# The float64 weights' conversion in an attention, experts and gated layer kernel: other steps, other buffers, other engines for its low part

## The chip, the cores and the metric

One NeuronCore of a Trainium2 chip runs the whole program. The metric is the device time of one execution in microseconds (us); the median of several is compared. The engines are PE (TensorE, matmuls; PEld is its weight load), DVE (VectorE), ACT (ScalarE), POOL (GpSimd) and SP (SyncE, which here only issues transfers). Each works through its own queue in order.

## What is computed

Three layers follow each other: attention with a window of 32 (in half of the heads with a stride of 4), a mixture of eight experts of which each of the 2304 tokens uses two, and a gated layer.

```python
def reference(**kwargs):
    ...
    attn_out = _attn_ref(**attn_kwargs)
    B, H, S, D = attn_out.shape
    x = np.ascontiguousarray(attn_out.transpose(0, 2, 1, 3)).reshape(B * S, H * D)
    x = _moe_ref(x=x, **moe_kwargs)
    return _moe2_ref(x=x, **moe2_kwargs)

def _moe2_ref(x, w_gate, w_val, w_out):
    g = x @ w_gate
    silu = g * (1.0 / (1.0 + np.exp(-g)))
    val = x @ w_val
    return (silu * val @ w_out).astype(np.float32)
```

The gated layer's three weights (512 x 1536 twice and 1536 x 512) arrive as float64. Every fp32 product is made of float32r parts: a high and a low one of each operand, and three matmuls.

## The kernel before

The order of the work is written by hand: each engine's queue holds its instructions in the order in which the program issues them. Attention comes first (36 units), then the expert layer, then the gated layer.

**The expert layer's steps.** `segs` cuts the experts' slots into 11 segments of 256, 256, 384, 384, five times 640, 384 and 256 slots; each has 8 steps, one for each 128 of the hidden columns, so there are 88 steps, and `moe_step(i)` issues one. Steps 16 to 31 are the segments of 384 slots, steps 32 to 71 the five of 640, steps 72 to 79 the next of 384. In a step

- SP loads the raw weights for step i+5 (line 156). There are three raw buffers, so this load waits until `wlo` of step i+2 is made.
- PE makes the first product (line 636) into bank A (steps of 640 slots have this one bank; those of 384 use A and B in turn), and then the second product of step i-1 (line 675).
- ACT makes hhi, the high part of the first product (line 648), then DVE makes hlo (line 649). The next step's first product needs the bank that both read.
- ACT makes whi (line 162) and DVE wlo (line 164), the weights' parts for step i+2.
- In the first steps of a segment POOL gathers rows of x for the next one (line 579, four gathers a step), and from its third step on, one block in each, DVE turns a block (line 585, "the transpose"), ACT makes xth (line 599) and DVE xtl (line 601). A segment of 640 slots has five such steps.

**The conversion.** The float64 weights are turned into float32r parts beside the expert layer, in 36 blocks of 128 x 512. From step 32 (`CV0`) on each step runs one `cv_tick(t)`, which does six stages for six blocks: load r (SP, line 739); clear what is below the least normal number (ACT three times, lines 753 to 756, and a POOL product, line 757, which gives cvw); one tick later cv_parts, four bit operations on DVE, which cut the 32-bit words into h, the high part, and c, the next bits (lines 763 to 766); then cv_hi: two more DVE operations (u, the power of two of h, line 772, and c with that exponent, line 773), ACT's copy hr of h (line 774) and SP's store of hr (line 778); then cv_sub: POOL makes c - u (line 794); then cv_lo: ACT's copy lr, scaled (line 784), and SP's store (line 788). The ticks run in steps 32 to 74. The conversion's pool lies on the right side of SBUF, where the routing's pool was until step 31. The stored parts are loaded again for the gated layer from step 80 on (`load_w2`, line 725).

Of the kernel before, what the change touches and what calls it, by code (L numbers as in the profile page):

```python
# [20 lines left out]
N, DM, E, FF, F2 = 2304, 512, 8, 1024, 1536  # L21
NT = N // 128          # token tiles
NB = S // 64           # query blocks of one sequence
SEG = S // 4           # positions of one residue class
NA = N // 128          # most slot blocks of one expert
CAP = 640              # slots of one expert on the straight path
EARLY = 256            # first slots of experts 0 and 1, filled by batches 0 and 1 only
LOW = 384              # tokens of one block of the last layer
ID0 = 1024
# [11 lines left out]
def attn_moe_glu_kernel(ctx, tc, qT, kT, vB, cst, wgn, noise, wm, wz, out):  # L41
# [16 lines left out]

    # rows of x by token, then rows of y by slot (block, expert, row); a token with a slot past the
    # straight path finds its combined row in the place of its x  # L60
    zd = dr.tile([N + NA * E * 128, DM], F32, name="zd")
# [21 lines left out]

    # ------------------------------------------------------------ loads
    qt, kt, vt = {}, {}, {}
# [12 lines left out]

    # dense work for the array while the first loads are on their way
    fill = gp.tile([128, 512], BF16, tag="g_ob", bufs=1, name="fill")  # L100
# [43 lines left out]

    # ------------------------------------------------------------ expert weights
    segs = [(0, 0, EARLY), (1, 0, EARLY), (0, EARLY, CAP), (1, EARLY, CAP)] \
# [18 lines left out]

    # ------------------------------------------------------------ attention
    units = []
# [63 lines left out]
    def pieces(subs):  # L231
        """(partition, type, first token, step, count) of the rows of a unit"""
        res = []
        for sub, (t, j) in enumerate(subs):
            p = j * 64
            while p < j * 64 + 64:
                if t == 0:
                    n = j * 64 + 64 - p
                    tok, st = p, 1
                else:  # L240
                    n = min(j * 64 + 64, (p // SEG + 1) * SEG) - p
                    tok, st = 4 * (p % SEG) + p // SEG, 4
                q0 = sub * 64 + p - j * 64
                if res and res[-1][1] == t and res[-1][2] + res[-1][4] * st == tok:
                    res[-1][4] += n
                else:
                    res.append([q0, t, tok, st, n])
                p += n
        return res
# [32 lines left out]

    # ------------------------------------------------------------ gating and routing
    groups = [(0, 4), (4, 9), (9, 13), (13, 18)]
# [7 lines left out]
    def regroup(o, src):  # L292
        """row 32 t + c of src to the rows 32 g + c of o's part t, for all g"""
        for t in range(4):
            T.matmul(o[:, t, :], lhsT=sel[:, t, :], rhs=src,
                     start=True, stop=True, skip_group_check=True)
# [244 lines left out]

    # the routing's small instructions, a few at a time between other work
    NEXT = "next"
# [22 lines left out]

    # ------------------------------------------------------------ expert layers
    xgt, xth, xtl, hps, hh_, hl_, yps = {}, {}, {}, {}, {}, {}, {}

    # column 4 p + k of a row belongs on partition p of chunk k: either PE turns a block of rows, or the  # L570
    # rows come in quarters, quarter g of the tokens 32 t + c on partition 32 g + c, and DVE turns 32 x 32
    def quarters(z):
# [8 lines left out]
    def turned(g, quarter, o=None):  # L581
        """a block of rows with its columns on partitions, [partition, chunk, row]"""
        if quarter:
# [10 lines left out]
    def parts(src, hi, lo, quarter, eng=V):  # L594
        """its two parts, on ACT and then on another engine"""
        how = "p k (t q) -> p k t q" if quarter else "p (k t) q -> p k t q"
# [92 lines left out]

    # ------------------------------------------------------------ emission: attention  # L690
    def att_step(i, turn):
# [3 lines left out]
        if i in FIRST_X:  # L695
            # the score bank has room for it
            tx = trans_x(0, FIRST_X.index(i), sT[i + 1][:, :, 192:448].rearrange("p a (c q) -> p a c q", c=2))
            next(tx)
# [32 lines left out]

    # the gated layer's weights, split once into two float32r parts
    cs = [{} for _ in range(3 * NK)]
# [14 lines left out]
    def cv_zero(n):  # L748
        if wide:
# [3 lines left out]
            A.activation(f, w1.bitcast(F32), AF.Abs)  # L753
            # 1 from the least normal number on, else 0
            A.activation(f, f, AF.Relu, scale=-2.0 ** 40, bias=least[0])
# [3 lines left out]
    def cv_parts(n):  # L759
        if wide:  # L760
            w0, w1 = cs[n]["r"][:, 0:1024:2], cs[n]["w"]
            h, c = cv_tile(n, "h", 2), cv_tile(n, "c", 3)
            V.tensor_scalar(h, w1, 3, 0x3FFFF000, op0=OP.logical_shift_left, op1=OP.bitwise_and)
            V.tensor_scalar(c, w1, 14, 0x7FC000, op0=OP.logical_shift_left, op1=OP.bitwise_and)
            V.scalar_tensor_tensor(h, w1, -0x40000000, h, op0=OP.bitwise_and, op1=OP.bitwise_or)
            V.scalar_tensor_tensor(c, w0, 18, c, op0=OP.logical_shift_right, op1=OP.bitwise_or)

    def cv_hi(n):
        hr = cv_tile(n, "hr", 2 if wide else 3, F32R)
        if wide:  # L770
            u, c, h = cv_tile(n, "u", 3), cs[n]["c"], cs[n]["h"]
            V.tensor_scalar(u, h, -0x800000, None, op0=OP.bitwise_and)
            V.scalar_tensor_tensor(c, h, -0x800000, c, op0=OP.bitwise_and, op1=OP.bitwise_or)
            A.activation(hr, h.bitcast(F32), AF.Copy)
        else:
            A.activation(hr, cs[n]["r"], AF.Copy)
        f, q = divmod(n, 3)
        SP.dma_start(whd[f, :, q * 512:q * 512 + 512], hr.bitcast(F32))

    def cv_lo(n):  # L780
        lr = cv_tile(n, "lr", 2, F32R)
        if wide:
            u = cs[n]["u"].bitcast(F32)
            A.activation(lr, u, AF.Copy, scale=2.0 ** -11)
        else:
            V.tensor_tensor(lr, cs[n]["r"], cs[n]["hr"].bitcast(F32), op=OP.subtract)
        f, q = divmod(n, 3)
        SP.dma_start(wld[f, :, q * 512:q * 512 + 512], lr.bitcast(F32))
        cs[n] = None

    def cv_sub(n):
        if wide:
            u, c = cs[n]["u"].bitcast(F32), cs[n]["c"].bitcast(F32)
            G.tensor_tensor(u, c, u, op=OP.subtract)

    def cv_tick(t):
        for d, fn in ((6, cv_lo), (5, cv_sub), (4, cv_hi), (3, cv_parts), (2, cv_zero), (0, cv_load)):
            if 0 <= t - d < 3 * NK:
# [34 lines left out]
    DVE_SEGS = (3, 11)  # L833
    CV0 = 32
    least = []
    pools = {}

    def moe_step(i):
        s, f = steps[i]
        last = s == len(segs) - 1  # L840
        load_raw(i + 5)
        if i == CV0:
            cv = pools["cv"] = st_cv.enter_context(tc.tile_pool(name="cv", bufs=1, side="right", reuse_waits="tile"))
            least.append(cv.tile([128, 1], F32, name="least"))
# [41 lines left out]
        go(5)  # L886
        if i == CV0 - 1:
            assert not route
            st_gate.close()
        if CV0 <= i:  # L890
            if i <= CV0 + 3 * NK + 6:
                cv_tick(i - CV0)
                if i == CV0 + 3 * NK + 6:
                    st_cv.close()
        list(tx)
# [37 lines left out]

    # ------------------------------------------------------------ emission: experts
    route.append([routing(3), True])
# [7 lines left out]

    # ------------------------------------------------------------ slots past the straight path
    rv = nc.values_load(most[0:1, 0:1], min_val=0, max_val=NA)
    with tc.If(rv > CAP // 128):  # L946
        with tc.tile_pool(name="ov", bufs=1) as ov:
            # rows that no expert computes
            none = ov.tile([128, E, DM], F32, name="none")
# [48 lines left out]

    # ------------------------------------------------------------ gated layer
    wp = ctx.enter_context(tc.tile_pool(name="wp", bufs=1))  # L1000
# [4 lines left out]
    def glu_gv(i):  # L1005
        b, f = st2[i]
        xh, xl = x2t[b]
        p = gvp[i] = bank2("AB"[i % 2])
        # what comes last from DVE or DRAM is used last
        parts = [(wh2[f], xh), (wh2[f], xl), (wl2[f], xh)] if i else [(wh2[f], xh), (wl2[f], xh), (wh2[f], xl)]  # L1010
# [19 lines left out]
    def glu_out(i):  # L1030
# [10 lines left out]
        if f == NK - 1:  # L1041
            for j in range(3):
                # the very last rows leave in two halves
                cut = (0, 256, 512) if b == NBLK - 1 and j == 2 else (0, 512)
# [111 lines left out]
```

## Time and profile before

| | |
|---|---|
| runs | 1083.07, 1078.17, 1081.59 us; median 1081.59 |
| the profiled execution | its span is 1085.7 us, 17127 instructions; no other time is given for it |
| PE busy | 1030.4 us (95%) |
| DVE busy | 667.9 us (62%) |
| ACT busy | 486.7 us (45%) |
| POOL busy | 441.3 us (41%) |
| chain that ended last | PE 42%, with all others under half a per cent |

The shares are means over the three layers, which have different limits, so the expert layer has to be read by itself: by windows of time, by the waits in it, and by the starts of an instruction that comes once in each step. Times in the trace are counted from the span's start. A row of the timeline gives start, duration, engine, line and operation, and in brackets the idle time of the engine before it and what ended it. A line of the page that sums instructions gives their count, the total and the mean in ns. An operation that stands behind a lock counts as busy.

### The profile page before, as it was taken

The numbers are of one execution on the slowest core, as the hardware profiler recorded it, in microseconds if no ns is written. First come the engines' busy times: TensorE is split into PE (matmuls) and PEld (weight loads), VectorE is DVE, ScalarE is ACT, GpSimd is POOL, SyncE is SP. The second block draws the span as 40 slices with busy tenths as digits, with TensorE's granted clock in tenths as the row PEclk, the third lists the DMA queues.
The fourth block names the chain that finished last, engine by engine and source line by source line (L and its number), as shares of the span: only waits on it lengthen the run. The fifth ranks groups of instructions, "written<-read, shape, count | busy, mean of one in ns | idle before, by whom it ended". The sixth has DMA issues, their size and how long they took to land. (4 is left out here: it accounts for less than half of the span.)

```text
span 1085.7 us, 17127 instructions
## 1 busy us (share of the span) xinstructions
PE 1030.4 (95%) x6561; PEld 923.5 (85%) x6562; DVE 667.9 (62%) x1223; ACT 486.7 (45%) x909; POOL 441.3 (41%) x389
## 2 busy tenths in 40 slices
PE   7888989999998888988999999999999999999998
PEld 5676779999987877877789899999999999999997
DVE  3468777674999999998995634434335344244222
ACT  4666644454767766676664422223223222122111
POOL 0014156741688576785761247724315116000000
PEclk9888999999999998998999999999999999999999
DMA  7777346654577676775769668511101101100000
GB/s 234 222 225 231 109 141 217 190 180 157 186 237 240 201 263 190 248 250 185 247 202 327 185 221 293 193 49 27 54 11 37 42 10 43 36 1 1 30 1 29
DMA packets 59526, 161.34 MB, mean 149 GB/s; under 512 B 10032, under 2 KB 16560, under 8 KB 58672
## 3 DMA queue, kind: packets, MB, share of 16 engines
q1 hardware_dynamic: 46736, 121.27, 35.0%
q0 software_dynamic: 12560, 38.82, 11.0%
q8 instruction: 52, 0.85, 0.3%
q14 instruction: 34, 0.28, 0.1%
q10 hardware_dynamic: 144, 0.13, 0.0%
HBM read 121.37 MB, written 38.80 MB: 148 GB/s over the span
## 5 line engine op out<-in xcount | busy, mean ns | idle before, releaser
L579 POOL DMA_INDIRECT yg<-zd,row x126 | 124.6, 989 | 200.8 <-DVE yg L820 117.4
L579 POOL DMA_INDIRECT xg<-zd,idx x139 | 163.9, 1179 | 58.5 <-issue 32.5
L636 PE MATMUL bA<-xth,whi 128*128 128x320 f32 (+2 forms) x452 | 119.2, 322 | 32.6 <-DVE hlo L649 32.4
L164 DVE TENSOR_TENSOR wlo<-raw,whi 128x1024 fp32r<-128x1024 f32 x80 | 112.7, 1408 | 12.9 <-ACT whi L162 12.8
L636 PEld LDWEIGHTS bA<-xth,whi 128*128 128x128 f32 x452 | 80.9, 194 | 46.0 <-DVE hlo L649 43.0
L636 PE MATMUL bA<-xtl,whi 128*128 128x320 f32 (+2 forms) x452 | 115.9, 315 | 0.0
L636 PE MATMUL bA<-xth,wlo 128*128 128x320 f32 (+2 forms) x452 | 115.7, 314 | 0.0
L1023 DVE TENSOR_TENSOR t<-bB,ex 128x384 f32<-128x384 f32 x36 | 20.1, 557 | 134.4 <-ACT ex L1021 134.4
L162 ACT ACTIVATE whi<-raw 128x1024 fp32r<-128x1024 f32 x88 | 92.7, 1053 | 3.4 <-DMA raw<-in_wm 3.4
L757 POOL TENSOR_TENSOR cvw<-r,cvw 128x512 f32<-128x512 f32 x36 | 58.5, 1625 | 84.8 <-issue 46.9
L648 ACT ACTIVATE hhi<-bA 128x640 fp32r<-128x640 f32 (+2 forms) x73 | 42.2, 578 | 98.4 <-PE bA L636 98.1
L636 PEld LDWEIGHTS bA<-xtl,whi 128*128 128x128 f32 x452 | 81.0, 194 | 1.2 <-DVE xtl L601 0.2
L636 PEld LDWEIGHTS bA<-xth,wlo 128*128 128x128 f32 x452 | 80.5, 193 | 0.0
L649 DVE SCALAR_TENSOR_TENSOR hlo<-bA,hhi 128x640 fp32r<-128x640 f32 (+2 forms) x73 | 48.6, 666 | 51.9 <-ACT hhi L648 51.9
L1027 ACT ACTIVATE th<-t 128x384 fp32r<-128x384 f32 x72 | 37.8, 524 | 90.3 <-DVE t L1024 90.3
L1021 ACT ACTIVATE ex<-bB 128x384 f32<-128x384 f32 x36 | 17.7, 492 | 135.0 <-PE bB L1015 135.0
L1023 DVE TENSOR_TENSOR t<-bA,ex 128x384 f32<-128x384 f32 x36 | 19.9, 554 | 83.5 <-ACT ex L1021 83.5
L1028 DVE TENSOR_TENSOR tl<-t,th 128x384 fp32r<-128x384 f32 x72 | 40.3, 559 | 42.6 <-ACT th L1027 42.6
L599 ACT ACTIVATE xth<-xg 128x512 fp32r<-128x512 f32 x33 | 38.0, 1152 | 63.4 <-DVE xg L585 63.4
L1015 PE MATMUL bA<-x2h,wh 128*128 128x384 f32 x288 | 56.6, 338 | 0.5 <-PEq L946 0.3
L1021 ACT ACTIVATE ex<-bA 128x384 f32<-128x384 f32 x36 | 17.7, 492 | 87.6 <-PE bA L1015 86.5
L1015 PE MATMUL bB<-x2h,wh 128*128 128x384 f32 x288 | 56.4, 337 | 0.0
(232 smaller groups left out, 2639.2 us busy)
## 6 DMA issues: line engine op xcount, KB each, us to landing
raw<-in_wm SPq DMA_DIRECT2D x88, 512.0 KB, 4.2
r<-in_wz SPq DMA_DIRECT2D x36, 512.0 KB, 5.9
zd<-y SPq DMA_DIRECT2D x40, 256.0 KB, 5.4
whd<-cvhr SPq DMA_DIRECT2D x36, 256.0 KB, 4.7
wld<-cvlr SPq DMA_DIRECT2D x36, 256.0 KB, 4.7
wh<-whd POOLq DMA_DIRECT2D x12, 768.0 KB, 8.6
wl<-wld POOLq DMA_DIRECT2D x12, 768.0 KB, 8.8
v<-in_vB SPq DMA_DIRECT2D x8, 877.5 KB, 8.7
```

The source lines that it names most:

```text
L162: A.activation(whi[i], raw[i], AF.Copy)
L164: eng.tensor_tensor(wlo[i], raw[i], whi[i].bitcast(F32), op=OP.subtract)
L579: G.indirect_dma_start(out=g, out_offset=None, in_=src, in_offset=bass.IndirectOffsetOnAxis(ap=ix, axis=0))
L599: A.activation(hi, src, AF.Copy)
L636: T.matmul(hp[:, q, 0:cw], lhsT=wt[:, ws], rhs=xt[:, c, q * cw:q * cw + cw], start=c == 0 and j == 0, stop=c == 3 and j == 2)
L648: A.activation(a3, hp, AF.Relu)
L649: V.scalar_tensor_tensor(l3, hp, 0.0, a3.bitcast(F32), op0=OP.max, op1=OP.subtract)
L757: G.tensor_tensor(f, w1.bitcast(F32), f, op=OP.mult)
L1015: T.matmul(p[:, q, 0:LOW], lhsT=w[:, ws], rhs=x[:, c, :], start=c == 0 and j == 0, stop=c == 3 and j == 2, skip_group_check=True)
L1023: V.tensor_tensor(t, p[:, 0, 0:LOW], ex, op=OP.mult)
L1027: A.activation(a, t, AF.Copy)
L1028: V.tensor_tensor(l, t, a.bitcast(F32), op=OP.subtract)
```

## The change

The conversion does the same for each block with other instructions. Five bit operations on DVE, all in cv_parts: u is made there, and c keeps its bits as an integer. cv_hi no longer copies h: h itself is stored, and ACT turns c into a float, scaled (cf). cv_lo multiplies cf by u on POOL and writes lr; its store moves to a stage of its own, one tick later, cv_end. h has three buffers in place of two, c two in place of three. The ticks are spread: the first five lie in steps 17, 20, 23, 26 and 29, the other 38 in steps 32 to 76, five in each six steps (there is none in 35, 41, 47, 53, 59, 65 and 71). The pool moves to the left side of SBUF, where the attention's was.

```diff
     def cv_parts(n):
         if wide:
             w0, w1 = cs[n]["r"][:, 0:1024:2], cs[n]["w"]
-            h, c = cv_tile(n, "h", 2), cv_tile(n, "c", 3)
+            h, c, u = cv_tile(n, "h", 3), cv_tile(n, "c", 2), cv_tile(n, "u", 3)
...
+            V.tensor_scalar(u, h, -0x800000, None, op0=OP.bitwise_and)
     def cv_hi(n):
-        hr = cv_tile(n, "hr", 2 if wide else 3, F32R)
         if wide:
-            u, c, h = cv_tile(n, "u", 3), cs[n]["c"], cs[n]["h"]
-            V.tensor_scalar(u, h, -0x800000, None, op0=OP.bitwise_and)
-            V.scalar_tensor_tensor(c, h, -0x800000, c, op0=OP.bitwise_and, op1=OP.bitwise_or)
-            A.activation(hr, h.bitcast(F32), AF.Copy)
+            hr = cs[n]["h"].bitcast(F32)
+            cf = cv_tile(n, "f", 2, F32)
+            A.activation(cf, cs[n]["c"], AF.Copy, scale=2.0 ** -34)
...
-        SP.dma_start(whd[f, :, q * 512:q * 512 + 512], hr.bitcast(F32))
+        SP.dma_start(whd[f, :, q * 512:q * 512 + 512], hr)
     def cv_lo(n):
         lr = cv_tile(n, "lr", 2, F32R)
         if wide:
-            u = cs[n]["u"].bitcast(F32)
-            A.activation(lr, u, AF.Copy, scale=2.0 ** -11)
+            G.tensor_tensor(lr, cs[n]["f"], cs[n]["u"].bitcast(F32), op=OP.mult)
...
+    def cv_end(n):
         f, q = divmod(n, 3)
-        SP.dma_start(wld[f, :, q * 512:q * 512 + 512], lr.bitcast(F32))
+        SP.dma_start(wld[f, :, q * 512:q * 512 + 512], cs[n]["lr"].bitcast(F32))
         cs[n] = None
-    def cv_sub(n):
-        if wide:
-            u, c = cs[n]["u"].bitcast(F32), cs[n]["c"].bitcast(F32)
-            G.tensor_tensor(u, c, u, op=OP.subtract)
+    CV_LAST = 6
     def cv_tick(t):
-        for d, fn in ((6, cv_lo), (5, cv_sub), (4, cv_hi), (3, cv_parts), (2, cv_zero), (0, cv_load)):
+        for d, fn in ((CV_LAST, cv_end), (5, cv_lo), (4, cv_hi), (3, cv_parts), (2, cv_zero), (0, cv_load)):
...
-    CV0 = 32
+    CVS = [17, 20, 23, 26, 29] + [32 + round(1.2 * j) for j in range(3 * NK + CV_LAST - 4)]
...
-        if i == CV0:
-            cv = pools["cv"] = st_cv.enter_context(tc.tile_pool(name="cv", bufs=1, side="right", reuse_waits="tile"))
+        if i == CVS[0]:
+            cv = pools["cv"] = st_cv.enter_context(tc.tile_pool(name="cv", bufs=1, reuse_waits="tile"))
...
-        if CV0 <= i:
-            if i <= CV0 + 3 * NK + 6:
-                cv_tick(i - CV0)
-                if i == CV0 + 3 * NK + 6:
-                    st_cv.close()
+        if i in CVS:
+            cv_tick(CVS.index(i))
+            if i == CVS[-1]:
+                st_cv.close()
```

First place: DVE's queue in a step of 640 slots that has a transpose and a block. Before:

```order
L649 SCALAR_TENSOR_TENSOR hlo<-bA,hhi 128x640
L585 STREAM_TRANSPOSE xg<-xg 128x4x4x32
L772 TENSOR_SCALAR cvu<-cvh 128x512
L773 SCALAR_TENSOR_TENSOR cvc<-cvh,cvc 128x512
L763 TENSOR_SCALAR cvh<-cvw 128x512
L764 TENSOR_SCALAR cvc<-cvw 128x512
L765 SCALAR_TENSOR_TENSOR cvh<-cvw,cvh 128x512
L766 SCALAR_TENSOR_TENSOR cvc<-r,cvc 128x512
L601 TENSOR_TENSOR xtl<-xg,xth 128x4x128
L164 TENSOR_TENSOR wlo<-raw,whi 128x1024
L649 SCALAR_TENSOR_TENSOR hlo<-bA,hhi 128x640
```

The same place with the change, with step 35 ahead of it, which has no tick:

```order
L649 SCALAR_TENSOR_TENSOR hlo<-bA,hhi 128x640
L585 STREAM_TRANSPOSE xg<-xg 128x4x4x32
L601 TENSOR_TENSOR xtl<-xg,xth 128x4x128
L164 TENSOR_TENSOR wlo<-raw,whi 128x1024
L649 SCALAR_TENSOR_TENSOR hlo<-bA,hhi 128x640
L585 STREAM_TRANSPOSE xg<-xg 128x4x4x32
L764 TENSOR_SCALAR cvh<-cvw 128x512
L765 TENSOR_SCALAR cvc<-cvw 128x512
L766 SCALAR_TENSOR_TENSOR cvh<-cvw,cvh 128x512
L767 SCALAR_TENSOR_TENSOR cvc<-r,cvc 128x512
L768 TENSOR_SCALAR cvu<-cvh 128x512
L601 TENSOR_TENSOR xtl<-xg,xth 128x4x128
```

A block has one DVE instruction less, and all five belong to the same block; step 35 has none.

Second place: DVE's queue at step 26, of 384 slots, with the change (before, xtl is followed by hlo at once):

```order
L649 SCALAR_TENSOR_TENSOR hlo<-bA,hhi 128x384
L585 STREAM_TRANSPOSE xg<-xg 128x4x4x32
L164 TENSOR_TENSOR wlo<-raw,whi 128x1024
L601 TENSOR_TENSOR xtl<-xg,xth 128x4x128
L764 TENSOR_SCALAR cvh<-cvw 128x512
L765 TENSOR_SCALAR cvc<-cvw 128x512
L766 SCALAR_TENSOR_TENSOR cvh<-cvw,cvh 128x512
L767 SCALAR_TENSOR_TENSOR cvc<-r,cvc 128x512
L768 TENSOR_SCALAR cvu<-cvh 128x512
L649 SCALAR_TENSOR_TENSOR hlo<-bB,hhi 128x384
```

The first block's five instructions stand ahead of step 27's hlo; the second block's stand likewise at step 29.

Third place: POOL's queue in two steps with gathers, before:

```order
L794 TENSOR_TENSOR cvu<-cvc,cvu 128x512
L757 TENSOR_TENSOR cvw<-r,cvw 128x512
L579 DMA xg<-zd,idx_86 128x128 x4
L794 TENSOR_TENSOR cvu<-cvc,cvu 128x512
L757 TENSOR_TENSOR cvw<-r,cvw 128x512
```

and with the change:

```order
L785 TENSOR_TENSOR cvlr<-cvf,cvu 128x512
L757 TENSOR_TENSOR cvw<-r,cvw 128x512
L579 DMA xg<-zd,idx_86 128x128 x4
L785 TENSOR_TENSOR cvlr<-cvf,cvu 128x512
L757 TENSOR_TENSOR cvw<-r,cvw 128x512
```

The product for lr stands where the subtraction stood, ahead of the one that gives cvw.

## Rows read from the trace of the kernel before

**Rows 1.** Windows: us, busy of PE, PEld, DVE, ACT, POOL, clock, DMA, GB/s

```profile
400.00:500.00 100.00, 86.35 (x450) 77.25 (x451) 96.38 (x116) 65.36 (x95) 69.21 (x53) 0.93 0.68 220
420.00:440.00 20.00, 15.56 (x74) 14.18 (x73) 17.23 (x23) 10.57 (x16) 8.91 (x6) 0.83 0.54 165
```

**Rows 2.** Waits from 280 to 565 us: total, times, longest

```profile
PEld bA L636 <- DVE hlo L649: 38.0, 22, 4.9
```

**Rows 3.** DVE line 649 (hlo): its forms, then starts in the timeline

```profile
L649 DVE SCALAR_TENSOR_TENSOR hlo<-bA,hhi x73: 409/809/826, 123.8 to 620.0; 128x640 fp32r<-128x640 f32 x40, 128x256 fp32r<-128x256 f32 x18, 128x384 fp32r<-128x384 f32 x15
...
264.16 0.82 DVE L649 SCALAR_TENSOR_TENSOR hlo<-bA,hhi 128x640 fp32r<-128x640 f32 x1 [4.77 <-ACT hhi L648]
...
284.98 0.82 DVE L649 SCALAR_TENSOR_TENSOR hlo<-bA,hhi 128x640 fp32r<-128x640 f32 x1 [0.21 <-ACT hhi L648]
...
374.15 0.81 DVE L649 SCALAR_TENSOR_TENSOR hlo<-bA,hhi 128x640 fp32r<-128x640 f32 x1
...
440.24 0.82 DVE L649 SCALAR_TENSOR_TENSOR hlo<-bA,hhi 128x640 fp32r<-128x640 f32 x1 [1.81 <-ACT hhi L648]
...
562.58 0.81 DVE L649 SCALAR_TENSOR_TENSOR hlo<-bA,hhi 128x640 fp32r<-128x640 f32 x1
```

**Rows 4.** Groups by line on DVE, 200 to 285 us, mostly without conversion

```profile
L164 DVE TENSOR_TENSOR wlo<-raw,whi 128x1024 fp32r<-128x1024 f32 x17 | 20.6, 1213 | 2.5 <-ACT whi L162 2.3
L585 DVE STREAM_TRANSPOSE xg<-xg 128x512 f32<-128x512 f32 x9 | 10.0, 1116 | 0.0
L601 DVE TENSOR_TENSOR xtl<-xg,xth 128x512 fp32r<-128x512 f32 x9 | 9.7, 1072 | 2.1 <-ACT xth L599 1.5
...
L765 DVE SCALAR_TENSOR_TENSOR cvh<-cvw,cvh 128x512 int32<-128x512 int32 x2 | 1.4, 683 | 0.0
...
L764 DVE TENSOR_SCALAR cvc<-cvw 128x512 int32<-128x512 int32 x2 | 0.8, 418 | 0.0
```

**Rows 5.** Groups by line on DVE, 280 to 560 us, beside the conversion

```profile
L164 DVE TENSOR_TENSOR wlo<-raw,whi 128x1024 fp32r<-128x1024 f32 x34 | 56.7, 1666 | 0.0
L601 DVE TENSOR_TENSOR xtl<-xg,xth 128x512 fp32r<-128x512 f32 x21 | 32.7, 1558 | 0.0
L766 DVE SCALAR_TENSOR_TENSOR cvc<-r,cvc 128x512 int32<-128x512 int32 x34 | 30.9, 910 | 0.0
L772 DVE TENSOR_SCALAR cvu<-cvh 128x512 int32<-128x512 int32 x35 | 29.2, 834 | 0.0
...
L773 DVE SCALAR_TENSOR_TENSOR cvc<-cvh,cvc 128x512 int32<-128x512 int32 x35 | 27.0, 773 | 0.0
L765 DVE SCALAR_TENSOR_TENSOR cvh<-cvw,cvh 128x512 int32<-128x512 int32 x34 | 25.3, 745 | 0.0
L764 DVE TENSOR_SCALAR cvc<-cvw 128x512 int32<-128x512 int32 x35 | 25.0, 715 | 0.0
...
L763 DVE TENSOR_SCALAR cvh<-cvw 128x512 int32<-128x512 int32 x35 | 14.8, 423 | 0.0
```

**Rows 6.** Timeline, DVE's wlo and POOL's two products in the same 4 us

```profile
386.80 3.98 DVE L164 TENSOR_TENSOR wlo<-raw,whi 128x1024 fp32r<-128x1024 f32 x1
...
387.11 1.31 POOL L794 TENSOR_TENSOR cvu<-cvc,cvu 128x512 f32<-128x512 f32 x1
...
388.36 1.32 POOL L757 TENSOR_TENSOR cvw<-r,cvw 128x512 f32<-128x512 f32 x1
```

**Rows 7.** Timeline of the same step: ACT's hhi, PE's last matmul of the second product

```profile
387.94 0.70 ACT L648 ACTIVATE hhi<-bA 128x640 fp32r<-128x640 f32 x1 [3.70 <-PE bA L636]
...
390.94 0.39 PE L675 MATMUL bf<-whi,hlo 128*128 128x512 f32 x1
```

**Rows 8.** Timeline, hlo of steps 27 and 28 (384 slots)

```profile
229.14 0.56 DVE L649 SCALAR_TENSOR_TENSOR hlo<-bB,hhi 128x384 fp32r<-128x384 f32 x1 [0.35 <-ACT hhi L648]
...
233.33 0.56 DVE L649 SCALAR_TENSOR_TENSOR hlo<-bA,hhi 128x384 fp32r<-128x384 f32 x1 [0.30 <-ACT hhi L648]
```

**Rows 9.** Tile of lr: its 36 stores' time from issue to landing

```profile
DMA to landing us min/median/max: 4.1/4.7/13.8
```

More of the change, by code (lines that the diff above doesn't have):

```diff
@@ L766, in cv_parts @@
             V.scalar_tensor_tensor(c, w0, 18, c, op0=OP.logical_shift_right, op1=OP.bitwise_or)
+            V.tensor_scalar(u, h, -0x800000, None, op0=OP.bitwise_and)
     def cv_hi(n):
-        hr = cv_tile(n, "hr", 2 if wide else 3, F32R)
+        f, q = divmod(n, 3)
         if wide:
-            u, c, h = cv_tile(n, "u", 3), cs[n]["c"], cs[n]["h"]
-            V.tensor_scalar(u, h, -0x800000, None, op0=OP.bitwise_and)
-            V.scalar_tensor_tensor(c, h, -0x800000, c, op0=OP.bitwise_and, op1=OP.bitwise_or)
-            A.activation(hr, h.bitcast(F32), AF.Copy)
+            hr = cs[n]["h"].bitcast(F32)
+            cf = cv_tile(n, "f", 2, F32)
+            A.activation(cf, cs[n]["c"], AF.Copy, scale=2.0 ** -34)
         else:
+            hr = cv_tile(n, "hr", 3, F32R)
             A.activation(hr, cs[n]["r"], AF.Copy)
-        f, q = divmod(n, 3)
-        SP.dma_start(whd[f, :, q * 512:q * 512 + 512], hr.bitcast(F32))
+            hr = hr.bitcast(F32)
+        SP.dma_start(whd[f, :, q * 512:q * 512 + 512], hr)
     def cv_lo(n):
@@ L886, in moe_step @@
         go(5)
-        if i == CV0 - 1:
+        if i == 31:
             assert not route
             st_gate.close()
-        if CV0 <= i:
-            if i <= CV0 + 3 * NK + 6:
-                cv_tick(i - CV0)
-                if i == CV0 + 3 * NK + 6:
-                    st_cv.close()
+        if i in CVS:
+            cv_tick(CVS.index(i))
+            if i == CVS[-1]:
+                st_cv.close()
         list(tx)
```

## Prediction

> **What bounds the kernel now.** I read four views in this order. First the windows: between 400 and 500 us DVE is busy for 96.38 of 100 us and PE for 86.35, and in the 20 us from 420 the granted TensorE clock has a mean of 0.83 [rows 1]. So in this stage the array is not the limit; its clock even falls to 1.2 GHz for a part of it, after PE has been waiting. Second the waits: what PE's weight loads wait for there is hlo, the last DVE instruction before the next step's matmuls, 38.0 us in 22 waits [rows 2]. Third, the starts of hlo on DVE, one per step [rows 3]. The row of forms says that there are 40 steps of 640 slots (steps 32 to 71); the last starts at 562.58, and the row at 284.98 is the sixth, step 37. From 264.16 to 284.98 three steps take 20.82 us, 6.94 each: that is PE's own pace. From step 37 to step 71 there are 34 steps in 277.6 us, where 34 x 6.94 is 236.0. **The excess is 41.6 us**, and it is all that a relief of DVE can give back here. The lower clock is a part of it. Behind this stage the chain of waits is PE alone, so time saved here reaches the end.
>
> Fourth, the price of DVE's instructions, without and with the conversion. Alone (200 to 285 us) wlo takes 1213 ns, the transpose 1116, xtl 1072, a one-tensor bit operation 418 and a two-tensor one 683 [rows 4]. Beside the conversion the means are 1666 for wlo, 1558 for xtl, and up to 910 for the bit operations [rows 5]. One row shows why: a wlo of 3.98 us has two GpSimd TENSOR_TENSORs of 1.31 and 1.32 us inside it [rows 6], and 1.21 + 2.63 is 3.84. Summed over rows 5 (mean less the time alone, times count) DVE loses 64 us in 34 blocks, each with two such GpSimd operations: 0.94 us for each. I call this the lock.
>
> The Trainium skill (SBUF — State Buffer, "SBUF: two separate sides") says that DVE and GpSimd share one pair of ports as an exclusive lock, held for a whole instruction, while the other fully blocks. Rows 6 agree with it.
>
> **The change, part by part.** *DVE.* A block had six bit operations and has five: line 773 leaves, 35 times 773 ns, 27.0 us [rows 5]. Of 36 blocks, six no longer lie in steps 35 to 71, but in 26, 29, 32, 33, 34 and 72. The other five groups of rows 5 sum to 125.2 us for 35 blocks, 3.58 each: 21.5 us more leaves the slow stage. Together that is 48.5, more than 41.6, so on the average DVE stops being the limit. If a step were an average, all 41.6 us would go.
>
> It isn't. hlo of a step can't start before PE has made that step's first product, so an idle DVE can't work ahead; it can only be late, by some 1.9 us, before PE stands: ACT's hhi ends at 388.64, hlo would be done 0.82 later, and PE has work until 391.33 [rows 7]. So I count steps with a transpose and a block: 0.82 + 1.12 + 1.07 + 1.21 + 3 x 0.42 + 2 x 0.68 = 6.84 us, and two locks. With the old block this rule gives 6.84 + 0.68 + 1.88 = 9.40, 2.46 over 6.94; five in a row less the 1.9 are 10.4 us per expert. Measured from 374.15 to 440.24, eight steps, is 66.1 less 55.5: 10.6 [rows 3]. The rule holds.
>
> Now for the new order. The pause of one step in six falls on 35, 41, 47, 53, 59, 65 and 71; steps three to seven of an expert have the transpose (three steps for the last of the five). So experts 4, 6 and 7 each have a run of three such steps (36 to 38, 50 to 52, 60 to 62) and single ones that the 1.9 us hides; the one at steps 64 to 71 has a run of three; the one at 40 to 47 has its pauses outside and five in a row. For the lock I take 0.8: a little under 0.94, because DVE now stands idle in the pauses and in the steps without a transpose, where an operation on GpSimd costs nothing. Each such step is then 6.84 + 1.6 - 6.94 = 1.5 over. Three in a row leave 4.5 - 1.9 = 2.6, five leave 5.6: 4 x 2.6 + 5.6 = **16 us stay**. With 0.94 it is 20.8, with 0.6 it is 9.2.
>
> *Two early blocks* at steps 26 and 29, in the 384-slot steps with a transpose. DVE has only 0.35 us of idle time in such a step of 4.19 us [rows 8]. A block and a lock put it 2.62 + 0.8 - 0.35 = 3.07 behind. With two banks in turn hlo is wanted later, by the end of the next first product: 4.19 less hhi (0.70 in its 640 form, rows 7, so no more) less 0.56 is 2.9 us of room. The first block loses 0.2; three steps win back 1.05, and the second block brings 3.07 again: 2.0. **2.2 us lost**, between 1.8 and 3.2 by locks of 0.6 and 1.31. The blocks at 32 to 34 cost nothing: at step 34 DVE stands idle for 4.77 us [rows 3].
>
> *ACT* makes one conversion (cf) in place of two copies (hr, lr): less by one copy a block, off the path, zero. That an int32 input costs the same I bound by zero and by one copy more, which would be the work of before. *GpSimd* keeps two TENSOR_TENSORs a block; the new one multiplies where the old one subtracted, and the two kinds in rows 6 take 1.31 and 1.32, so its own cost is unchanged. *SP* issues the same transfers; whd waits for a DVE instruction of the step before instead of ACT's copy, and the five early loads are passed by raw loads with room to spare. *Other buffers*: the conversion's space is that of the attention, long finished at step 17; zero.
>
> **Sum:** 41.6 - 16 - 2.2 = 23.4 us less. The profiled span is 1085.7, 4.1 above the median of 1081.6; I take the difference from both, since the stage is the same: 1062 for a profiled span, **1058.0 for a run**.
>
> **Rivals.** *A, every lock is paid in full.* Both kernels have GpSimd's two operations next to each other on its queue, and a DVE instruction behind them stands for 2.6 us. Each step with transpose and block is then 6.84 + 2.62 - 6.94 = 2.5 over: runs of three leave 5.7, five 10.7, the three singles 0.6 each: 35, and 3.2 for the early blocks. Only 3.4 is won: 1078, within half a per cent. Against it stands the mean of 0.94 over a DVE queue that was never idle. The rule of the Trainium skill's page SBUF — State Buffer, taken for every operation, gives this sum.
>
> *B, the buffers of lr (slower).* lr has two buffers. Before, ACT filled them; now GpSimd does, one tick earlier, so its multiplication stands until the store of two blocks ago, issued one step before, has landed. Behind it on GpSimd is the masking product for the next block, which DVE wants. From the end of a DVE step: landing, 1.31 and 1.32; DVE comes for it 6.94 + 0.82 + 1.12 = 8.9 later. So the store has some 6.2 us; the median is 4.7, the longest 13.8 [rows 9]. A late one is first covered by the 1.9 us. Over some 34 blocks the 23.4 are used up at a landing of 6.2 + 1.9 + 0.7 = 8.8; from there on each microsecond costs 34. At 9.5: 1105. For it: raw, both stores and r leave SP together, and the early steps add to that. Against: the median.
>
> *C, nothing is left over.* GpSimd's operations fall beside hlo, the transposes and idle time, and every run is absorbed: 1081.6 - 41.6 = 1040. Against it: five steps in a row are over 6.94 at any lock above 0.05.
>
> *D, the change does not relieve DVE:* the removed operation's time is refilled by longer locks and the lower clock stays: 1080.
>
> **How the numbers follow.** About 0.5% (5.4 us) is what a measurement of this kernel can tell from no change. Forecast (1046 to 1070, lock between 0.5 and 1.1): 0.70. A 0.08, B 0.07, C 0.10, D 0.05. Faster is the forecast, C and 0.03 of A: 0.83. Same is the rest of A and D: 0.10. Slower is B: 0.07. Since a lock of 0.6 to 0.94 alone spans 1051 to 1064 (41.6 less 9.2 and 1.8, or less 20.8 and 2.5), and half of A and C lie outside, the range is 1042 to 1076.
>
> **What would show it.** In the profile after: DVE between 300 and 500 us under 95% busy; waits of PE for hlo cut from 38.0 us to about 15; hlo starts 6.94 apart in pauses and in steps without a transpose, 8 to 9 in runs with it; the block's operations five; steps 26 to 31 longer by 2 us together. The stage from step 37 to 71 should take 252 us. B would show as waits of GpSimd for the landing of wld of several us each, and DVE waiting for cvw. I am wrong if the stage is shorter but the end isn't, or if the early steps lose more than 5 us.

## The result and the profile after

The changed kernel takes 1066.51 us (median of 4 runs, 1065.70 to 1069.68) beside 1082.33 for the kernel before; the medians lie 15.8 us apart. The ratio on record is 0.9846 (95% interval 0.9809 to 0.9883). It isn't the quotient of these two medians, which is 0.9854, and it makes 16.7 us. 23.4 us were forecast; the time lies in the stated range. The profiled execution has a span of 1063.9 us, where that of before had 1085.7: 21.8 us less. I read this trace first and come back to the 5 to 6 us between the two differences.

The windows of the changed kernel, columns as in [rows 1]:

```profile
300.00:400.00 100.00, 96.98 (x544) 87.89 (x543) 74.35 (x106) 64.26 (x90) 71.37 (x58) 1.00 0.74 248
400.00:500.00 100.00, 95.60 (x523) 85.75 (x522) 79.55 (x105) 61.12 (x85) 64.20 (x54) 0.98 0.71 227
240.00:260.00 20.00, 16.40 (x79) 13.90 (x78) 15.92 (x20) 10.43 (x16) 11.15 (x11) 0.91 0.51 170
```

DVE is no longer busy throughout (79.55 us of 100 where it was 96.38), PE is at 95.60 in place of 86.35, and the clock's dips are shorter. But in the 20 us from 240, where PE had no idle time before, it has some now, and the clock falls too.

The waits of the same stage (262 to 545 us), which answer to [rows 2]:

```profile
POOL cvlr L785 <- DMA wld<-cvlr: 38.3, 12, 6.5
...
DVE cvh L764 <- POOL cvw L757: 27.0, 15, 4.6
...
PEld bA L636 <- DVE hlo L649: 12.8, 8, 2.4
```

What PE waits for hlo went from 38.0 to 12.8 us. Two waits are new: GpSimd's product for lr stands for the landing of a store of lr, and DVE stands for cvw, the masked word.

The starts of hlo at steps 26, 32, 37 and 71, which answer to [rows 3]:

```profile
223.85 0.56 DVE L649 SCALAR_TENSOR_TENSOR hlo<-bA,hhi 128x384 fp32r<-128x384 f32 x1 [2.01 <-ACT hhi L648]
...
257.71 0.82 DVE L649 SCALAR_TENSOR_TENSOR hlo<-bA,hhi 128x640 fp32r<-128x640 f32 x1 [1.26 <-ACT hhi L648]
...
291.00 0.82 DVE L649 SCALAR_TENSOR_TENSOR hlo<-bA,hhi 128x640 fp32r<-128x640 f32 x1 [0.77 <-ACT hhi L648]
...
540.05 0.82 DVE L649 SCALAR_TENSOR_TENSOR hlo<-bA,hhi 128x640 fp32r<-128x640 f32 x1 [1.35 <-ACT hhi L648]
```

Steps 37 to 71 take 249.05 us, 28.55 less than 277.60. Steps 26 to 32 take 33.86; before it was 26.81, between these two rows of the kernel before, so 7.05 is lost there:

```profile
224.89 0.56 DVE L649 SCALAR_TENSOR_TENSOR hlo<-bA,hhi 128x384 fp32r<-128x384 f32 x1 [2.01 <-ACT hhi L648]
...
251.70 0.82 DVE L649 SCALAR_TENSOR_TENSOR hlo<-bA,hhi 128x640 fp32r<-128x640 f32 x1 [3.63 <-ACT hhi L648]
```

Steps 71 to 80 take 1.3 more, with the last ticks in them; the rest, 1.6 less, is mostly the start, where step 26 comes 1.0 earlier. The sum is the 21.8.

DVE's groups in the stage, 265 to 545 us, which answer to [rows 5]; the lines 764 to 768 are now the block's five operations:

```profile
L164 DVE TENSOR_TENSOR wlo<-raw,whi 128x1024 fp32r<-128x1024 f32 x39 | 55.1, 1412 | 0.5
...
L601 DVE TENSOR_TENSOR xtl<-xg,xth 128x512 fp32r<-128x512 f32 x23 | 26.4, 1150 | 3.6 <-ACT xth L599 3.6
...
L767 DVE SCALAR_TENSOR_TENSOR cvc<-r,cvc 128x512 int32<-128x512 int32 x32 | 23.0, 720 | 0.0
L766 DVE SCALAR_TENSOR_TENSOR cvh<-cvw,cvh 128x512 int32<-128x512 int32 x32 | 23.0, 719 | 0.0
L768 DVE TENSOR_SCALAR cvu<-cvh 128x512 int32<-128x512 int32 x32 | 16.8, 524 | 0.0
L764 DVE TENSOR_SCALAR cvh<-cvw 128x512 int32<-128x512 int32 x31 | 13.9, 449 | 27.1 <-POOL cvw L757 27.0
L765 DVE TENSOR_SCALAR cvc<-cvw 128x512 int32<-128x512 int32 x31 | 13.2, 427 | 0.0
```

xtl is at 1150 ns where it was 1558, wlo at 1412 in place of 1666. Summed as in the prediction (mean less the time alone of [rows 4], times count) the lock is 16 us in place of 64, and the 27.0 us before line 764 are in no row of before.

A step of the new kind, step 50, in the timeline of DVE and GpSimd:

```profile
383.63 1.10 DVE L585 STREAM_TRANSPOSE xg<-xg 128x512 f32<-128x512 f32 x1
388.88 0.43 DVE L764 TENSOR_SCALAR cvh<-cvw 128x512 int32<-128x512 int32 x1 [4.15 <-POOL cvw L757]
...
393.23 0.81 DVE L649 SCALAR_TENSOR_TENSOR hlo<-bA,hhi 128x640 fp32r<-128x640 f32 x1
...
386.28 1.30 POOL L785 TENSOR_TENSOR cvlr<-cvf,cvu 128x512 fp32r<-128x512 f32 x1 [3.88 <-DMA wld<-cvlr]
387.54 1.31 POOL L757 TENSOR_TENSOR cvw<-r,cvw 128x512 f32<-128x512 f32 x1
```

GpSimd stands 3.88 us for the store, then makes lr, then cvw; DVE stands 4.15 us for cvw, and the next hlo starts 10.3 us after the last (382.89) in place of 6.94. Yet no DVE operation is stretched here: GpSimd's products ran while DVE stood. So the lock and this wait are paid with the same time, which is what the first experiment is about.

### The profile page after: what moved, and what is told of

Read it like the earlier page. It is cut to its first block, busy times and chain, and to the rows that moved or that the text cites. A ratio compares the mean times of both kernels' runs of the same rounds, so it can differ in the third digit from the quotient of the medians.

```text
span 1063.9 us, 17015 instructions
## 1 busy us (share of the span) xinstructions
PE 1021.8 (96%) x6562; PEld 918.0 (86%) x6562; DVE 607.7 (57%) x1187; ACT 468.3 (44%) x873; POOL 431.3 (41%) x389
## 3 DMA queue, kind: packets, MB, share of 16 engines
q1 hardware_dynamic: 46736, 121.27, 35.3%
## 5 line engine op out<-in xcount | busy, mean ns | idle before, releaser
L579 POOL DMA_INDIRECT xg<-zd,idx x139 | 154.7, 1113 | 48.4 <-issue 32.1
L636 PE MATMUL bA<-xth,whi 128*128 128x320 f32 (+2 forms) x452 | 115.7, 314 | 13.8 <-DVE hlo L649 13.8
L164 DVE TENSOR_TENSOR wlo<-raw,whi 128x1024 fp32r<-128x1024 f32 x80 | 110.0, 1375 | 8.9 <-ACT whi L162 8.4
L785 POOL TENSOR_TENSOR cvlr<-cvf,cvu 128x512 fp32r<-128x512 f32 x36 | 55.0, 1529 | 62.2 <-DMA wld<-cvlr 44.1
L1021 ACT ACTIVATE ex<-bB 128x384 f32<-128x384 f32 x36 | 17.7, 492 | 135.6 <-PE bB L1015 135.6
L757 POOL TENSOR_TENSOR cvw<-r,cvw 128x512 f32<-128x512 f32 x36 | 52.7, 1465 | 40.5 <-ACT cvw L756 29.1
L1015 PE MATMUL bA<-x2h,wl 128*128 128x384 f32 x288 | 56.4, 337 | 0.0
```

Of the source, the lines that this page charges most:

```text
L164: eng.tensor_tensor(wlo[i], raw[i], whi[i].bitcast(F32), op=OP.subtract)
L579: G.indirect_dma_start(out=g, out_offset=None, in_=src, in_offset=bass.IndirectOffsetOnAxis(ap=ix, axis=0))
L636: T.matmul(hp[:, q, 0:cw], lhsT=wt[:, ws], rhs=xt[:, c, q * cw:q * cw + cw], start=c == 0 and j == 0, stop=c == 3 and j == 2)
L757: G.tensor_tensor(f, w1.bitcast(F32), f, op=OP.mult)
L785: G.tensor_tensor(lr, cs[n]["f"], cs[n]["u"].bitcast(F32), op=OP.mult)
L1015: T.matmul(p[:, q, 0:LOW], lhsT=w[:, ws], rhs=x[:, c, :], start=c == 0 and j == 0, stop=c == 3 and j == 2, skip_group_check=True)
```

## Experiments

Each is compared with runs of the kernel before beside it. "Stage" is the time from hlo of step 37 to hlo of step 71, "early" from step 26 to step 32, in each kernel's profiled execution; steps 32 to 37 take 33.3 us but in "the change, again" (35.3), "masking product first" (35.6) and "ticks by hand" (34.7). "Lock" and "wait for cvw" are taken from DVE's groups as above, for "before, profiled again" over the same steps (294 to 574 us).

| kernel | ratio to before, interval | early | stage | lock | wait for cvw |
|---|---|---|---|---|---|
| before | 1 | 26.8 | 277.6 | 64 | 0 |
| before, profiled again | | 30.1 | 272.6 | 64 | 0 |
| the change | 0.9846 (0.9809 to 0.9883) | 33.9 | 249.1 | 16 | 27.0 |
| the change, again | 0.9846 (0.9801 to 0.9890) | 32.9 | 252.4 | 20 | 24.1 |
| lr in three buffers | 0.9876 (0.9850 to 0.9903) | 33.3 | 250.8 | 44 | 7.8 |
| first ticks earlier | 0.9847 (0.9819 to 0.9876) | 28.6 | 249.3 | 16 | 28.8 |
| instructions only | 0.9921 (0.9895 to 0.9947) | 26.8 | 261.8 | 12 | 43.7 |
| steps only | 0.9958 (0.9940 to 0.9976) | 31.9 | 262.3 | 51 | 0 |
| masking product first | 0.9763 (0.9724 to 0.9803) | 32.8 | 238.0 | 20 | 3.3 |
| ticks by hand | 0.9784 (0.9748 to 0.9821) | 27.4 | 245.5 | 14 | 17.7 |
| masking first, early ticks | 0.9676 (0.9643 to 0.9708) | 26.8 | 237.9 | 26 | 2.6 |
| masking first, all from step 32 | 0.9758 (0.9722 to 0.9795) | 26.8 | 246.2 | 29 | 9.4 |
| hr copied again | 0.9847 (0.9806 to 0.9888) | 32.6 | 249.5 | 15 | 24.1 |
| before, its subtraction last | 0.9897 (0.9862 to 0.9933) | 26.8 | 261.8 | 47 | 0 |

"Before, profiled again", "the change, again", "masking product first" and "ticks by hand" ran beside each other at a time when the kernel before took 1098 us and the gated layer alone some 7 us more; they are read by their ratios. The record gives these four and the last four the same chip number, and beside the last four the kernel before took 1084 us, so the chip's number doesn't explain it.

### lr in three buffers

```diff
-        lr = cv_tile(n, "lr", 2, F32R)
+        lr = cv_tile(n, "lr", 3, F32R)
```

> lr has three buffers instead of two. Theory 'buffer': the store of lr that GpSimd waits for (44.1 us, 14 times in the changed kernel's trace) keeps the masking product back, and DVE waits for that (27.0 us, 15 times); without it both waits vanish, PE's waits for hlo in steps 37 to 71 shrink by half, and a run takes about 1060 us. Rival 'lock': the wait keeps GpSimd's two products apart; without it they stand back to back beside DVE, the lock (DVE's time over that alone, 20 us in the changed kernel, 65 before) rises to 40 or more, and a run takes 1068 to 1075 us.

The run takes 1070.62 us. The wait for cvw falls by 19.2 us and the lock rises by 28: with no store to wait for, GpSimd's two products stand beside working DVE operations again.

```profile
L768 DVE TENSOR_SCALAR cvu<-cvh 128x512 int32<-128x512 int32 x33 | 24.9, 754 | 0.0
L764 DVE TENSOR_SCALAR cvh<-cvw 128x512 int32<-128x512 int32 x32 | 21.3, 667 | 8.9 <-POOL cvw L757 7.8 <-DMA whd<-cvh 1.1
```

These rows of DVE's groups answer to 524 and 449 ns in the change. The rival "lock" holds for what happened; the stage, 250.8 in place of 249.1, says that it is nearly even.

### The first ticks earlier

```diff
-    CVS = [17, 20, 23, 26, 29] + ...
+    CVS = [15, 17, 19, 21, 23] + ...
```

> The first five ticks lie in steps 15, 17, 19, 21 and 23, so the two early blocks of DVE come in steps 21 and 23, which have no transpose, instead of 26 and 29. Theory 'early steps': the 7.05 us that steps 26 to 32 lost (33.86 us against 26.81 before) come from these two blocks among the transposes; they fall to under 2, and a run takes 1060 to 1062 us. Rival: the loss comes from GpSimd's queue (gathers standing behind a product that waits for ACT); then it stays at 4 or more, now at another step, and a run takes 1065 to 1068 us.

Early steps fall from 33.9 to 28.6 us, a loss of 1.8, as "early steps" has it; steps 16 to 26 give 0.6 of it back. Part of the rest is the rival's: three transposes of these steps still stand 0.3, 2.2 and 2.1 us for a gather. But the median is 1065.96, in the rival's range, and the ratio that of the change. The gain of 4.7 us is seen in the trace and not in the time, whose interval is 6 us wide. In the profiled executions the start takes most of it back: step 16 begins at 186.26 us here and at 182.64 in the change. This run alone doesn't settle the size.

### The new instructions alone, and the new steps alone

```diff
-    CVS = [17, 20, 23, 26, 29] + [32 + round(1.2 * j) for j in range(3 * NK + CV_LAST - 4)]
+    CVS = list(range(32, 32 + 3 * NK + CV_LAST + 1))
```

> The new instructions, ticks in each step from 32 to 74 as before. Theory 'instructions': most of the gain is from DVE's shorter block and the smaller lock, so the stage (steps 37 to 71; 277.6 us before, 249.1 changed) takes 252 to 258, the early loss of 7 us is gone, and a run takes about 1063 to 1068 us. Rival 'pauses': without a pause DVE stays the limit; the stage takes 265 to 272, and a run 1072 to 1078 us.

For the steps alone the kernel before got the list of steps and the pool on the left:

```diff
-    CV0 = 32
+    CVS = [17, 20, 23, 26, 29] + [32 + round(1.2 * j) for j in range(3 * NK + 2)]
```

> The old instructions and buffers' numbers, with the new steps and the pool on the left. Theory 'instructions': the stage takes 262 to 268 us, the early steps lose 7 to 10, and a run takes 1075 to 1081 us. Rival 'pauses': the stage takes about 255, and a run 1067 to 1072 us.

The first takes 1072.86 us, which lies in the range of "pauses" and not in that of "instructions"; its stage of 261.8 is between the two forecasts. The second takes 1079.12 us with a stage of 262.3, both as "instructions" has it; its early steps lose 5.0, less than the 7 to 10 forecast. The instructions alone win 0.8%, the steps alone 0.4% (with the early loss already in it), both 1.5%. Without pauses DVE stands 43.7 us for cvw: what the shorter block gives is partly lost in waiting for GpSimd.

### GpSimd's masking product ahead of the product for lr

```diff
-        for d, fn in ((CV_LAST, cv_end), (5, cv_lo), (4, cv_hi), (3, cv_parts), (2, cv_zero), (0, cv_load)):
+        for d, fn in ((CV_LAST, cv_end), (4, cv_hi), (3, cv_parts), (2, cv_zero), (5, cv_lo), (0, cv_load)):
```

> Within a tick GpSimd's masking product now comes ahead of the product for lr, so DVE no longer waits behind the landing of lr's store; two buffers of lr as in the change. Theory 'exchange' (from the run with three buffers: lock up by what the wait goes down): the waits of DVE for cvw fall from 27.0 us to under 8, the lock rises from 16 to 30 or more, the stage of steps 37 to 71 stays at 247 to 252 us, and a run takes 1063 to 1069 us. Rival 'buffer': the wait was a pure loss; the lock stays under 20, the stage takes 238 to 243 us, and a run takes 1056 to 1060 us.

Ratio 0.9763, some 0.8% under the change's repeat, which ran beside it. The stage takes 237.97 us, between these two starts of hlo, where PE's own pace is 236.0:

```profile
295.49 0.82 DVE L649 SCALAR_TENSOR_TENSOR hlo<-bA,hhi 128x640 fp32r<-128x640 f32 x1 [2.98 <-ACT hhi L648]
...
533.46 0.82 DVE L649 SCALAR_TENSOR_TENSOR hlo<-bA,hhi 128x640 fp32r<-128x640 f32 x1 [1.93 <-ACT hhi L648]
```

"Exchange", the theory that I had drawn from the three buffers, falls: the wait for cvw goes (24.1 to 3.3) and the lock stays at 20. The groups say where it now lies:

```profile
L164 DVE TENSOR_TENSOR wlo<-raw,whi 128x1024 fp32r<-128x1024 f32 x40 | 53.0, 1326 | 0.9 <-ACT whi L162 0.4
L764 DVE TENSOR_SCALAR cvh<-cvw 128x512 int32<-128x512 int32 x33 | 28.5, 863 | 3.8 <-POOL cvw L757 3.3 <-DMA whd<-cvh 0.5
```

Three quarters of it are in line 764, the block's first operation; wlo, xtl and the other four are within 0.12 us of their times alone. So it isn't the two buffers alone, which a third one replaces without a gain, but the order on GpSimd's queue that cost the change its time: the product that DVE needs stood behind one that nobody is in a hurry for. How much of the gain is the wait and how much the lock that didn't come in its place isn't shown; this order with three buffers of lr wasn't run. Counted from step 32, since steps 32 to 37 differ too, the gain up to step 71 is 8.8 us on the change's first profile (273.6 for 282.3) and 14.2 on its repeat.

### Ticks by hand

```diff
-    CVS = [17, 20, 23, 26, 29] + [32 + round(1.2 * j) for j in range(3 * NK + CV_LAST - 4)]
+    CVS = [13, 16, 17, 18, 21, 31, 32, 33, 35, 36, 37, 38, 39, 40, 41, 43, 44, 46, 47, 49, 50, 52, 53, 54, 55,
+           57, 58, 59, 60, 62, 63, 65, 66, 67, 68, 69, 71, 73, 76, 77, 78, 79]
```

> The changed kernel's instructions with a tick list by hand: steps 13, 16, 17, 18 and 21, none from 22 to 30, then two to six in a row with pauses (none in 34, 42, 45, 48, 51, 56, 61, 64, 70, 72, 74, 75), the last in 79. Theory 'early steps and runs': the early loss of 7 us is under 1.5, and shorter runs between the pauses keep the stage of steps 37 to 71 at 240 to 246 us; a run takes 1054 to 1060 us. Rival: what is won early comes back in the fuller stage (30 blocks in steps 35 to 71, no fewer than in the change); the stage takes 249 to 256, and a run takes 1062 to 1068 us.

Ratio 0.9784. Early steps take 27.4 and the stage 245.5, both as "early steps and runs" has it. Steps 80 to 87 take 27.9 us where all the others have 21 to 22: something of the late ticks is paid there. Which instruction it is I did not try.

### Two repeats

> The kernel before, profiled once more: how far its stages differ between executions. Theory 'the start differs': step 16 begins up to 5 us earlier or later, and the stage of steps 37 to 71 takes 274 to 280 us again. Rival 'the stage differs': the first profile was a bad one, and the stage takes 268 to 273.

> The changed kernel, timed beside the others of this call: 1064 to 1069 us; in its profile the early steps 26 to 32 take 33 to 35 us and the stage of steps 37 to 71 takes 247 to 252 us again. If the first profile was a lucky one, the stage takes 254 or more.

In its second profile the kernel before begins step 16 at 189.8 us, 6.1 later than in its first, as the theory has it and by more. Its stage of 272.6 us is in the rival's range, its steps 16 to 32 take 75.6 where they took 68.0, and its lock is 64 again. The change repeats its ratio to the fourth digit, which is chance with an interval of 0.9801 to 0.9890, and its early steps to 1 us; its stage, 252.4, is a little over the range. Its median of 1079.67 isn't in the range, as everything took longer beside it. In the 23 runs of the kernel before beside the first four experiments the times go from 1078.43 to 1087.60 on one chip.

### Both improvements together

The order of "masking product first" with

```diff
-    CVS = [17, 20, 23, 26, 29] + ...
+    CVS = [13, 16, 17, 18, 21] + ...
```

> The order of e5 (GpSimd's masking product ahead of the product for lr) with the first five ticks in steps 13, 16, 17, 18 and 21, so the two early blocks of DVE lie in 18 and 21 and none in 26 and 29. Theory 'both add up': the early steps 16 to 32, 75 us in the change, take 69 to 70, the stage of steps 37 to 71 stays at 237 to 241, and the ratio to before is 0.970 to 0.973. Rival: the early blocks collide with the gathers there; steps 16 to 32 take 73 or more, and the ratio is that of e5, 0.976, or worse.

1048.47 us, ratio 0.9676, the fastest of all. Steps 16 to 32 take 68.3 us (19.08 up to step 20, 22.41 up to 26, 26.80 up to 32), as in the kernel before (68.0), and the stage 237.9. The waits from 262 to 545 us, beside 12.8 and 27.0 in the change:

```profile
DVE cvh L764 <- POOL cvw L757: 2.6, 6, 0.5
PEld bA L636 <- DVE hlo L649: 2.2, 2, 1.5
```

Its windows show a PE that is almost never idle, at the full clock:

```profile
300.00:400.00 100.00, 98.81 (x553) 89.36 (x551) 82.94 (x109) 65.18 (x91) 74.63 (x64) 1.00 0.76 252
400.00:500.00 100.00, 99.82 (x564) 91.30 (x565) 82.39 (x111) 65.75 (x91) 67.89 (x57) 1.00 0.77 251
```

### Masking product first, ticks in each step from 32

The order of "masking product first" and the list of "instructions only".

> The order of e5, with ticks in each step from 32 to 74 as before the change. Theory 'order': with GpSimd's wait for the store out of DVE's way, DVE has idle time to spare (55 us in e5's stage), so the pauses aren't needed: the stage takes 239 to 246 us against 261.8 with the change's order, steps 26 to 32 take 27, and the ratio is 0.970 to 0.978. Rival 'pauses': five steps with a transpose in a row stay too much; the stage takes 250 to 258, and the ratio is 0.982 to 0.990.

1057.36 us; the stage is 246.2, just over the upper end of "order", against 261.8 with the change's order. The pauses are worth 8 us of the stage, the order 11 (249.1 to 238.0) with pauses and 16 without. Here too most of the lock, 25 of 29 us, is in one row:

```profile
L764 DVE TENSOR_SCALAR cvh<-cvw 128x512 int32<-128x512 int32 x36 | 39.6, 1101 | 11.7 <-POOL cvw L757 9.4 <-DMA whd<-cvh 2.2
```

### hr copied again

```diff
-            hr = cs[n]["h"].bitcast(F32)
+            hr = cv_tile(n, "hr", 2, F32R)
+            A.activation(hr, cs[n]["h"].bitcast(F32), AF.Copy)
+            hr = hr.bitcast(F32)
```

> The changed kernel, but ACT copies h to hr again and hr is stored (h has two buffers). Theory: ACT's copy is covered, and the ratio stays at 0.983 to 0.988. Rival: one copy more a block on ACT makes hhi late (ACT waits 70 us for PE in the stage, so this would need a run of busy steps); the ratio rises to 0.990 or more.

1066.32 us, ratio 0.9847: ACT's copy is covered, and that hr is stored from h is worth nothing in time.

### The kernel before with its subtraction last

```diff
-        for d, fn in ((6, cv_lo), (5, cv_sub), (4, cv_hi), (3, cv_parts), (2, cv_zero), (0, cv_load)):
+        for d, fn in ((6, cv_lo), (4, cv_hi), (3, cv_parts), (2, cv_zero), (5, cv_sub), (0, cv_load)):
```

> The kernel before with only the order of GpSimd's two products turned round: the masking product first, then c - u. Theory 'store': in the kernel before nothing on GpSimd waits for a store, so the order is worth little: ratio 0.995 to 1.002, the stage 272 to 280 us. Rival 'order': it is the neighbourhood of the two products itself that costs DVE its time; the lock falls from 64 to 40 us or less, the stage to 262 or less, and the ratio is 0.988 or lower.

1074.93 us, ratio 0.9897: the theory "store" falls. Turning round two instructions of one queue wins 1% with the old instructions too, where no product waits for a store. The lock falls to 47 us, less than the rival said, and two thirds of it lie in one operation:

```profile
L772 DVE TENSOR_SCALAR cvu<-cvh 128x512 int32<-128x512 int32 x35 | 47.0, 1343 | 0.0
```

wlo is at 1341 ns and xtl at 1085 in this run (1666 and 1558 in [rows 5]). So there are two effects of the order: which DVE operations meet the products, and, in the change, who stands behind the store.

## Why the prediction was right in its direction and too large

**The bound.** That DVE sets the pace of steps 37 to 71, and that 41.6 us over PE's pace is all that can come back, held: the best stage is 237.9 us, 1.9 over 236.0.

**The stage.** 16 us were to stay; 13.1 stayed (16.4 in the repeat). The size was right, the account wasn't, so that it came out is luck. I had two locks of 0.8 us for each block, 54 us for 34 blocks, and the trace has 16 of lock and 27 of waiting for cvw. Nor is the loss where the sum put it, 5.6 us in the expert of steps 40 to 47 and 2.6 in each other: from step 40 on the experts lose 1.7, 3.9, 5.3 and 2.3 us (in the repeat 5.7, 2.4, 6.5 and 2.0), and the three steps 37 to 39 nothing. Where a block meets a transpose, hlo starts 6.9 to 10.7 us apart, not 8 to 9 throughout.

Rival B, which I gave 0.07 and only as a slowdown, was at work: GpSimd stood 12 times for a store, DVE 15 times for cvw, and three buffers take 19.2 of DVE's 27.0 us away. The landing of 4.6 us in the median is under the 6.2 that I allowed, counted from the end of wlo, and most stores are issued 0.5 us behind it. But in the first step of an expert five stores of y stand ahead on SP's queue, which I had not counted. Ahead of step 50, shown above, wlo ended at 375.68:

```profile
374.47 1.21 DVE L164 TENSOR_TENSOR wlo<-raw,whi 128x1024 fp32r<-128x1024 f32 x1
...
376.17 3.36 SPq L688 DMA_DIRECT2D zd<-y  x5
379.62 0.51 SPq L791 DMA_DIRECT2D wld<-cvlr  x1
```

GpSimd went on 6.66 us after this issue, and DVE stood for 4.15; its other long wait (4.55) follows the same way at step 58. Six others, of 1.0 to 2.3 us, come when gathers and lr's product stand right ahead of cvw on GpSimd's queue, without a wait for a store. B didn't make the kernel slower because the lock was paid in the same time (lr in three buffers).

**The early blocks.** 2.2 us were forecast, 7.05 and 6.1 measured; this term was mis-sized by 5, and by the prediction's own sign ("if the early steps lose more than 5 us") its account was wrong here. PE's timeline from 228 to 252 us has idle time of 0.84 and 1.37 us for wlo, 0.95 for hhi and 1.28 for hlo; I had counted hlo alone:

```profile
234.93 0.45 PE L636 MATMUL bB<-xth,wlo 128*128 128x384 f32 x1 [0.84 <-DVE wlo L164]
...
244.92 0.44 PE L636 MATMUL bB<-xth,wlo 128*128 128x384 f32 x1 [1.37 <-DVE wlo L164]
...
247.90 0.50 PE L675 MATMUL bc<-whi,hhi 128*128 128x512 f32 x1 [0.95 <-ACT hhi L648]
...
249.91 0.58 PE L675 MATMUL bc<-whi,hlo 128*128 128x512 f32 x1 [1.28 <-DVE hlo L649]
```

The clock of 0.91 over the 20 us from 240 is 1.8 us more by my estimate (20 times 0.09). And GpSimd's gathers, which ran ahead in the kernel before (the 20th of them starts at 190.51 there and at 215.73 here), stand behind the masking products, the first of which waits 25.10 us for ACT, so a transpose came late:

```profile
214.27 1.32 POOL L757 TENSOR_TENSOR cvw<-r,cvw 128x512 f32<-128x512 f32 x1 [25.10 <-ACT cvw L756]
...
242.65 1.14 DVE L585 STREAM_TRANSPOSE xg<-xg 128x512 f32<-128x512 f32 x1 [2.53 <-DMA xg<-zd,idx]
```

The order list ahead of the prediction showed these products among the gathers; I costed them at nothing there. With the early ticks of the best kernel the loss is 0.3.

**The sum.** "I take the difference from both, since the stage is the same" failed. The trace gives 21.8 us, near the 23.4; the runs give 16.7 by the ratio and 15.8 by the medians. (1081.6 less 23.4 is 1058.2; the 1058.0 is off by a rounding, and so is the 1064 of the range's working, which is 1063.) The profiled execution of the kernel before was a long one: its span of 1085.7 is at the top of what the 23 later runs show (a run's time is some 2 us over its span there, and the longest was 1087.6), while that of the change was the shortest of four. Its second profile has a stage 5.0 us shorter; set against that, the change wins 23.6 there and loses 7.05 and 1.3 elsewhere: 15.2, near what was measured. But that this is where the executions differ isn't shown: the same profile takes 7.6 us more in steps 16 to 32, and the start differs too, for step 16 begins between 182.3 and 189.8 us in kernels that are the same up to there.

**The rest.** ACT's copies at zero: shown (hr copied again; the conversion of an int32 input takes 623 ns, the copy took 621). Rival A, every lock in full, is out: 16 to 20 us of lock, where 2.62 for each of 33 blocks would be 86. C is out for the change, but with the masking product first 1.9 us are left of the 41.6. D is out: the lock fell from 64 to 16. Steps 71 to 80 lost 1.3 us that I had not counted.

## What to carry to other kernels

When an engine serves two consumers through one queue in order, put the instruction that somebody waits for ahead of the one that itself waits for a transfer: here this was worth 9 to 14 us between steps 32 and 71, more than the pauses (8). A wait that the profile shows need not be time that can be won, if another loss falls in it; take it away in two ways (a buffer, an order) before believing either. And a term that is won on one profiled execution is a term of that execution: look at how far the runs spread before carrying its last 5 us to a median.

## What the runs showed of the hardware that I had not expected

A DVE operation of one source (0.42 us alone) can cost 1.34 us on the average beside GpSimd's two products, while wlo and xtl around it take nearly their own times: which of them pays depends on what DVE issues when GpSimd starts, so the same 70 or so products cost 12 to 64 us (the 12 beside 43.7 us of DVE's waiting for cvw). Not every operation can pay: in all 14 profiles hlo of 640 slots takes 0.80 to 0.84 us and the transpose 1.09 to 1.17, although 235 of the one and 188 of the other lie over a GpSimd product for more than 0.4 us; a wlo of 1.21 us takes up to 4.26.

And the same kernel spreads over 9 us on one chip (1078.43 to 1087.60), with 14 us more at another time, 7 of them in the gated layer, whose work is the same. In those profiles PE isn't busy throughout there, as in the others: in the 100 us from 634 us of "masking product first" it is busy for 95.2 at a granted clock of 0.97. What it waited for the profile doesn't show.
